# One list schedule over fixed buffers for a two-half state-space and convolution kernel

## The chip, the cores and the metric

The kernel runs on one core of a Trainium2 chip. The metric is the device time of one execution in microseconds (us), the median of several runs. One more execution is taken with the hardware profiler; its rows are what is read below.

## The reference

The input `x` is 2048 tokens of 640 channels. Four layers follow one another, each on a layer-normalised `x` and added to `x`:

```python
x = x + _A_ref(_layernorm(x), ...)   # A1
x = x + _B_ref(_layernorm(x), ...)   # B1
x = x + _A_ref(_layernorm(x), ...)   # A2, same weights as A1
x = x + _B_ref(_layernorm(x), ...)   # B2, same weights as B1
# _A_ref: h_t = Lam_bar * h_(t-1) + B_bar u_t (complex, 640 states); y = 2 Re(C h) + Dskip * u
# _B_ref(q, k, v): kv = shift_conv4(k) * v; y = causal_conv(kv, ssm_k) + ssm_D * kv; return q * y
```

In `_B_ref` only `q` depends on `x`. The long convolution `y` depends on the inputs `B_k`, `B_v`, `B_ssm_k` alone, so it is computed once and used by B1 and B2.

## The kernel before

The program has two halves. The first half builds everything that does not depend on `x`; the second half is the four layers.

**First half.** `a_setup_tasks` makes the weights of the A layers: `BT0` (the input matrices transposed, by ten DMA transposes, `e_bt0`, L379 and L380), `BT1` (the same times a diagonal, 100 matmuls and 10 evacuations), `W0`, `W1` (20 small products from transposed `C`, L444 and L445) and `G0` (five products of 10 x 640 columns, L464). The diagonals `Ld`, `Fd` and `DS` are made on VectorE, one 128 x 128 block at a time (L327, L429, L845). `y_table_tasks` makes sine and cosine tables, `kv_tasks` the product `kv` (stored in DRAM as `kvd`), and `y_pass` the convolution of one fifth of the channels (`qd` = 0 to 4): two transforms in two stages each (A: L908, B: L930 to L935) for the kernel (`KA`, `KB`) and for `kv` (`VA`, `VB`), six products on VectorE (L984 to L989), two stages back (`IB`: L1008 and L1009, a DMA transpose L1021, `IA`: L1036), and a store to DRAM as `ysd`.

**Second half.** Tokens come in four chunks of 512. `ALayer.chunk` does one chunk of an A layer: mean and variance (`ln_stats`: row sums L1182, squares L494), normalisation into `u` (L511 on ScalarE or L513 on VectorE), a DMA transpose into `uT` (L538), 100 matmuls of 256 columns into `ab` (L553, L556, evacuated at L562), rotation (L575 to L577), two scans (L591), rotation back into `h` (L614 to L616), four output groups of matmuls (L636, 33,280 columns in all), and one VectorE operation each that adds the residual and sums the row (`e_xe`, L641). `b_chunk` does one chunk of a B layer: statistics, normalisation into `bu`, product with `Y` (L665), addition to `x` with the row sum (L667), or into `o` for the output (L670).

**What sets the order.** Each half is a list of tasks with an engine, an estimated cost and dependencies. `Sched.run` is a list scheduler that puts them into an order by rank. It runs once for each half, and the program is emitted in that order; the framework's own scheduler may still move instructions. Buffers are rings of tiles in memory pools. The pools of the first half are closed before those of the second half are opened over the same memory, so no tile of the second half can be written before the first half's tiles there are done with. All DMAs are issued from the SP queue, in one order.

Of the kernel before, what the change touches and what calls it, by code (L numbers as in the profile page):

```python
# [43 lines left out]
QORD = [0, 16] + list(range(1, 16))  # L44
QGRP = [(0, 4), (4, 8), (8, 12), (12, 16), (16, 17)]


class Task:
    __slots__ = ("name", "engs", "ests", "eng", "est", "deps", "emit", "idx", "start", "finish", "rank", "succ", "bias", "lat", "uses")

    def __init__(self, name, eng, est, deps, emit, idx, bias, lat, uses):
# [5 lines left out]
        self.start = self.finish = None  # L57
        self.rank = 0.0
        self.succ = []
        self.bias, self.lat = bias, lat  # L60
        self.uses = uses


class Slot:
    __slots__ = ("tile", "users", "ring", "left", "vis", "held", "num")

    def __init__(self, ring, num):
        self.num = num
# [12 lines left out]

class Ring:

    def __init__(self, bufs, alloc, in_order=True):
        self.alloc = alloc
        self.avail = [0.0] * bufs
        self.in_order = in_order
        self.made = self.given = 0

# [5 lines left out]
class Sched:  # L95
    LAT = {"pe": 0.2, "act": 0.25, "dve": 0.2, "pool": 0.3, "sp": 2.2, "xp": 2.0}

    debug = False

    def __init__(self):  # L100
        self.tasks = []

    def add(self, name, eng, est, deps, emit, bias=0.0, lat=None, uses=()):
        t = Task(name, eng, est, deps, emit, len(self.tasks), bias, lat, list(uses))
        for s in t.uses:
            s.users += 1
        self.tasks.append(t)
        return t

    def vis(self, d):  # L110
        return d.finish + (d.lat if d.lat is not None else self.LAT[d.eng])

    def run(self):
        tasks = self.tasks
        for t in tasks:
# [16 lines left out]
        eps = 1e-9  # L132

        def can(t):
            if rtime[t.idx] > now + eps:
                return False
            need = {}
            for s in t.uses:
                if not s.held:
                    need[s.ring] = need.get(s.ring, 0) + 1  # L140
                    if s.ring.in_order and s.num != s.ring.given + 1:
                        return False
            for r, n in need.items():
                if sum(1 for a in r.avail if a <= now + eps) < n:
# [3 lines left out]
        while len(order) < len(tasks):  # L148
            progressed = False
            for eng in sorted(eng_free):  # L150
# [39 lines left out]
        for t in order:  # L190
            t.emit(t.eng)
        span = max(t.finish for t in tasks)
        if self.debug:
            self.report(order, span)
        return span

    def report(self, order, span):
        engs = sorted({t.eng for t in order})
        print("[sched] span %.1f" % span, {e: round(sum(t.est for t in order if t.eng == e), 1) for e in engs})
        bk = 10.0  # L200
        for b in range(int(span / bk) + 1):
            row = []
            for e in engs:
                o = sum(max(0.0, min(t.finish, (b + 1) * bk) - max(t.start, b * bk)) for t in order if t.eng == e)
                row.append("%s %3.0f" % (e, 100 * o / bk))
            print("   %5.0f  " % (b * bk) + "  ".join(row))


def c_mm(n, k=1):
    return k * (n / 2400.0 + 0.003)  # L210


def c_act(n, sb=False):
    return (0.25 if sb else 0.22) + 0.00083 * n


def c_tt(n, slow=False):
    return 0.15 + (0.00104 if slow else 0.00053) * n
# [16 lines left out]
def make_consts(nc, pool):  # L235
# [5 lines left out]
    for nm, v in (("half_pi", HALF_PI), ("neg_pi", -PI_LO), ("pos_pi", PI_LO)):  # L241
# [9 lines left out]
def a_setup_tasks(S, nc, wp, sp, R_ps, consts, A_Lambda_re, A_Lambda_im, A_B_re, A_B_im, A_C_re, A_C_im, A_log_dt, A_Dskip):  # L251
# [12 lines left out]
    st = {}  # L264

    def tl(nm, shape, dt=F32):
        return sp.tile(shape, dt, tag=nm, name=nm)

    s_pp = R_ps.new()

    def e_pl(_):
        st["pb"] = tl("pl_b", [4 * NJ, P], BF)
        for v, vec in enumerate((A_Lambda_re, A_Lambda_im, A_log_dt, A_Dskip)):
            nc.sync.dma_start(out=st["pb"][NJ * v:NJ * (v + 1), :], in_=vec.rearrange("(j p) -> j p", p=P))
    t_pl = S.add("a_pl", "sp", 0.3, [], e_pl, bias=3000)

    def e_pt(_):
        pf = tl("pl_f", [4 * NJ, P])
        nc.vector.tensor_copy(pf[:], st["pb"][:])
        ps = s_pp.get()  # L280
        nc.tensor.transpose(ps[:, 0:4 * NJ], pf[:], consts["ident_f"][0:4 * NJ, 0:4 * NJ])
        st["pf"] = tl("pl", [P, 4 * NJ])
        nc.vector.tensor_copy(st["pf"][:], ps[:, 0:4 * NJ])
# [954 lines left out]
```

## Time and profile before

| | |
|---|---|
| median of 3 runs | 463.53 us (460.25 to 464.36) |
| the profiled execution | 462.58 us, of which the span from the first to the last instruction is 460.6 us |
| mean granted clock of TensorE | 0.914 of full speed |
| busy: PE, DVE, ACT, POOL | 349.6, 323.9, 244.9, 6.9 us |

In the rows PE is TensorE, PEld its weight load, DVE is VectorE, ACT is ScalarE, POOL is GpSimd and SP is the engine that issues DMAs; L12 is line 12 of the kernel. A row of the stretches gives for each engine the busy time in that stretch, then the granted clock and the share of the DMA engines.

### The profile page before, as it was taken

The page shows a single profiled execution, that of the slowest core. Times are in us where ns is not written, and L with a number is a line of the kernel's source. Part 1 is how long each engine was busy: PE and PEld are TensorE (multiplying, and loading weights), DVE is VectorE, ACT ScalarE, POOL GpSimd, SP SyncE. Part 2 cuts the span into 40 slices and gives each one's busy share as a digit, 9 for nine tenths or more (in the row PEclk, how much of TensorE's full clock was granted, in tenths as well). Part 3 has the DMA queues.
Part 4 walks back from the last instruction along what each step waited for, and adds up shares of the span by engine and source line. Part 5 has one row for each costly group of instructions (what it writes and reads, how often), then busy time and mean ns, then how long its engine had stood idle before and what let it go on. Part 6 is the DMA issues. An engine that isn't in the chain of part 4 may idle for free.

```text
span 460.6 us, 7946 instructions
## 1 busy us (share of the span) xinstructions
PE 349.6 (76%) x3303; PEld 256.2 (56%) x3330; DVE 323.9 (70%) x595; ACT 244.9 (53%) x380; POOL 6.9 (1%) x21
## 2 busy tenths in 40 slices
PE   0386777989888796049799529999997698999920
PEld 0153466988777653038645318876574475855510
DVE  4995657688787630022997715999699899699674
ACT  3643457889888451962203779521737453430734
POOL 5000000000000000000000000000000000000000
PEclk9998989999999799559989958999998699999985
DMA  6999995929735668051002153301301313030021
GB/s 143 249 177 240 237 218 98 178 49 193 144 60 112 129 115 280 30 96 20 0 1 58 43 128 58 58 1 58 59 1 57 57 58 58 2 114 1 30 85 57
DMA packets 118173, 43.25 MB, mean 94 GB/s; under 512 B 112117, under 2 KB 113402, under 8 KB 118138
## 3 DMA queue, kind: packets, MB, share of 16 engines
q1 hardware_dynamic: 118138, 42.75, 41.8%
q8 instruction: 26, 0.43, 0.4%
q14 instruction: 9, 0.07, 0.1%
HBM read 14.76 MB, written 7.86 MB: 49 GB/s over the span
## 4 chain that ended last, share of the span: by engine, by line
DVE 38%; ACT 13%; PE 13%; DMA 5%; issue 2%; ACTq 0%; SPq 0%
DVE g L591 10%; ACT junk L494 8%; DVE x L641 4%; PE ps L464 3%; DMA xb<-in_A_x_dram 3%; DVE bu L665 2%; PE ps L553 2%; DVE t L575 2%; DVE o L670 2%; DVE g L577 2%; DVE t L615 2%; DVE t L614 2%; DVE t L576 2%; DMA uT<-u 2%; PE ps L556 2%; DVE x L667 2%
## 5 line engine op out<-in xcount | busy, mean ns | idle before, releaser
L636 PE MATMUL ps<-W,h 128*128 128x512 bf16 (+1 forms) x632 | 98.1, 304 | 6.4 <-DVE h L616 5.9
L223 ACT ACTIVATE q<-ps 128x1024 bf16<-128x1024 f32 (+2 forms) x81 | 75.4, 1003 | 42.8 <-PE ps L935 19.2
L553 PE MATMUL ps<-uT,BT 128*128 128x256 bf16 x400 | 61.1, 287 | 42.1 <-DMA uT<-u 41.8
L494 ACT ACTIVATE junk<-x,nmean 128x640 bf16<-128x640 f32 x48 | 39.7, 827 | 75.9 <-DVE nmean L488 61.4
L636 PEld LDWEIGHTS <-h 128*128 128x128 bf16 x640 | 50.2, 99 | 42.6 <-DVE h L616 6.9
L553 PEld LDWEIGHTS <-BT 128*128 128x128 bf16 x400 | 40.8, 103 | 49.6 <-issue 22.7
L556 PE MATMUL ps<-uT,BT 128*128 128x256 bf16 x400 | 60.1, 284 | 0.0
L591 DVE TENSOR_TENSOR_SCAN g<-rtab,g 128x1290 bf16<-128x1290 f32 x16 | 44.8, 2833 | 0.0
L556 PEld LDWEIGHTS <-BT 128*128 128x128 bf16 x400 | 40.8, 102 | 6.1
L225 DVE CAST q<-ps 128x1024 bf16<-128x1024 f32 (+2 forms) x34 | 30.4, 929 | 17.2 <-PE ps L1009 10.4
L511 ACT ACTIVATE bu<-x,nmr,rstd 128x640 bf16<-128x640 f32 x26 | 23.5, 915 | 28.2 <-DVE x L667 18.4
L930 PE MATMUL ps<-q,Cf 128*128 128x128 bf16 x170 | 35.6, 222 | 3.5 <-DVE vT L872 2.8
L933 PE MATMUL ps<-q,NSf 128*128 128x128 bf16 x170 | 35.8, 222 | 0.0
L562 ACT ACTIVATE ab<-ps 128x1024 bf16<-128x1024 f32 (+1 forms) x24 | 20.8, 871 | 24.5 <-PE ps L556 24.4
L935 PE MATMUL ps<-q,Cf 128*128 128x128 bf16 x150 | 33.2, 221 | 0.0
L932 PE MATMUL ps<-q,Sf 128*128 128x128 bf16 x150 | 33.2, 221 | 0.0
L866 PE MATMUL ps<-kT,DS 128*128 128x512 bf16 x78 | 21.4, 431 | 14.4 <-DVE DS L845 11.3
L908 PE MATMUL ps<-FA,qx 128*128 128x256 bf16 x160 | 21.5, 276 | 9.1 <-DMA qx<-kvd 2.4
L636 PEld LDWEIGHTS <-uT 128*128 128x128 bf16 x240 | 19.8, 99 | 13.7 <-issue 0.5
L636 PE MATMUL ps<-G,uT 128*128 128x128 bf16 (+1 forms) x151 | 26.8, 297 | 0.5
L908 PEld LDWEIGHTS <-qx 128*128 128x128 bf16 x160 | 15.6, 99 | 13.9 <-issue 9.0
L866 PEld LDWEIGHTS <-DS 128*128 128x128 bf16 x80 | 8.5, 107 | 26.0 <-DVE DS L845 12.4
(218 smaller groups left out, 652.1 us busy)
## 6 DMA issues: line engine op xcount, KB each, us to landing
Y<-ysd SPq DMA_DIRECT2D x8, 640.0 KB
qx<-in_B_ssm_k_dram SPq DMA_DIRECT2D x5, 512.0 KB
kvd<-vT SPq DMA_DIRECT2D x5, 512.0 KB, 4.5
qx<-kvd SPq DMA_DIRECT2D x5, 512.0 KB, 4.7
ysd<-yq SPq DMA_DIRECT2D x5, 512.0 KB
xb<-in_A_x_dram SPq DMA_DIRECT2D x4, 640.0 KB, 4.0
out_dram<-o SPq DMA_DIRECT2D x8, 320.0 KB, 2.2
Bnat<-in_A_B_re_dram SPq DMA_DIRECT2D x1, 800.0 KB, 6.7
```

Source lines behind the costliest of these rows:

```text
L223: nc.scalar.activation(out, in_, ACT.Copy)
L225: nc.vector.tensor_copy(out, in_)
L494: nc.scalar.activation(junk[:], src(q), ACT.Square, bias=st["nmean"][:, q:q + 1], scale=1.0, accum_out=st["ssq"][:, q:q + 1])
L553: nc.tensor.matmul(pb[:, jj, c2, :], lhsT=aw["BT1"][:, c2, j, k, :], rhs=uT[:, k, 0:2, :].rearrange("p t i -> p (t i)"), start=(k == 0), s ...
L556: nc.tensor.matmul(pb[:, jj, c2, :], lhsT=aw["BT0"][:, c2, k, j * P:(j + 1) * P], rhs=uT[:, k, 2:4, :].rearrange("p t i -> p (t i)"), star ...
L591: nc.vector.tensor_tensor_scan(gv, rt, gv, 0.0, ALU.mult, ALU.add)
L636: nc.tensor.matmul(pc[:, o0:o1], lhsT=lh, rhs=rh, start=(n == 0), stop=(n == len(ops) - 1))
L908: nc.tensor.matmul(pa[:, o4, :], lhsT=s_x.get()[:, 4 * g + o4, :], rhs=T["FA"][:], start=True, stop=True)
L930: nc.tensor.matmul(ps[:, g, 0, :], lhsT=T["Cf"][:, q, :], rhs=are, start=True, stop=single)
L932: nc.tensor.matmul(ps[:, g, 0, :], lhsT=T["Sf"][:, q, :], rhs=A[:, 2 * q + 1, :], start=False, stop=True)
L933: nc.tensor.matmul(ps[:, g, 1, :], lhsT=T["NSf"][:, q, :], rhs=are, start=True, stop=single)
L935: nc.tensor.matmul(ps[:, g, 1, :], lhsT=T["Cf"][:, q, :], rhs=A[:, 2 * q + 1, :], start=False, stop=True)
```

## The change

- **One schedule.** All tasks of both halves go into one `Sched`. Its order is emitted under `manual_schedule()`, which keeps it as it is on each engine. The tasks of the first half have larger ranks (`S.base`), so a layer task goes ahead only where they leave an engine free.
- **Fixed buffers.** Nearly all tiles are views of 13 buffers of 2580 bf16 (`b5`) and 6 of 2580 f32 (`b10`), which are allocated once and shared by both halves. A ring now has a store and a cap; the scheduler picks the buffer.
- **Weights by PE.** `BT0` comes from 50 matmuls with the identity and 10 evacuations. The two `B` matrices and the first `ssm_k` are loaded by DMAs of the ACT queue.
- **GpSimd** makes the diagonals `Ld`, `Fd`, `DS`, `DD` (one operation for many blocks), the short chain of factors, and the tables `FA`, `HA`.
- **A1 residual on PE.** For A1, `x` is loaded a second time (`xr`, one buffer) and added by one more identity matmul per column part (16 x 640 columns). The row sum with the copy to `x` can then be on ACT or DVE.
- **Layer norm.** The mean and the standard deviation are scaled on ACT (L524, L534) and no longer on DVE. The last chunk of B2 is normalised one row group at a time.

```diff
 class Ring:
-    def __init__(self, bufs, alloc, in_order=True):
-        self.alloc = alloc
-        self.avail = [0.0] * bufs
+    def __init__(self, store, cap, view, in_order=True):
+        self.store, self.cap, self.view, self.in_order = store, cap, view, in_order
...
-        for t in order:
-            t.emit(t.eng)
...
+        with self.tc.manual_schedule():
+            for t in order:
+                t.emit(t.eng)
...
+    def diag(dst, scal, n):
+        nc.gpsimd.tensor_tensor(dst, ident[:, None, :].to_broadcast([P, n, P]), scal[:, :, None].to_broadcast([P, n, P]), ALU.mult)
...
-            nc.sync.dma_start_transpose(out=aw["BT0"][:, 0, k, :], in_=A_B_re[:, k * P:(k + 1) * P])
-            nc.sync.dma_start_transpose(out=aw["BT0"][:, 1, k, :], in_=A_B_im[:, k * P:(k + 1) * P])
...
+                for j in range(NJ):
+                    nc.tensor.matmul(pb[:, j, :], lhsT=s_B[c].get()[:, j, k * P:(k + 1) * P], rhs=ident[:], start=True, stop=True)
...
-        nc.vector.tensor_scalar(st["nmean"][:], sums(), -1.0 / D, None, ALU.mult)
+        nc.scalar.activation(st["nmean"][:], sums(), ACT.Copy, scale=-1.0 / D)
...
+        if reload is not None:
+            res_slot = reload[0]
+            t_xr = S.add(f"{nm}_xr", "sp", 0.4, [t_bp], reload[1], uses=[res_slot], xt=3.0)
...
+                    if reload is not None:
+                        ops = ops + [(ident[:], resid(q)[:, d0:d1], d0, d1)]
...
+                if reload is not None and eng == "act":
+                    nc.scalar.activation(s_x.get()[:, q, :], s_pc.get()[:, 0:D], ACT.Identity, accum_out=sums_out()[:, q:q + 1])
...
-        S.run()
-        early.close()
-
-
-    S = Sched()
-    with ExitStack() as a:
...
+        "b5": store(wp, NB5, "b5", [P, 2 * NJ * NC2], BF),
+        "b10": store(wp, 6, "b10", [P, 2 * NJ * NC2], F32),
...
+        "q1": Ring(b10, 2, lambda t: bfv(t, NQ * 2 * DQ)),
+        "q2": Ring(b10, 2, lambda t: bfv(t, NQ * 2 * DQ)),
+        "q3": Ring(b10, 2, lambda t: bfv(t, NQ * 2 * DQ)),
...
+        "xb": Ring(b5, 2, v4),
+        "xr": Ring(b5, 1, v4),
...
+        groups = [range(4)] if c < NCH - 1 else [[0], [1], [2], [3]]
```

The order of ScalarE where the two halves meet. Before, the last evacuations of `G` (a weight) and `yq` (the last convolution output) stand ahead of the first row sum of `xb` (chunk 0 of `x`):

```order
L223 ACTIVATE G_98<-ps 128x640
L223 ACTIVATE yq<-ps 128x16x64
L223 ACTIVATE G_98<-ps 128x640 x4
L1182 ACTIVATE junk,sums<-xb 128x640 x5
L494 ACTIVATE junk,ssq<-xb,nmean 128x640 x4
```

After, where the same weight `G` is evacuated (names that begin with `b_` are shared buffers; `b_5_87` holds chunk 0 of `x`, `b_1_96` and `b_5_100` hold spectra of the second and third fifth, `b_2_84` the first fifth's output):

```order
L240 ACTIVATE G_114<-ps_103 128x640
L1236 ACTIVATE junk,sums_1188<-b_5_87 128x640 x4
L524 ACTIVATE nmean_0_1215<-sums_1188 128x4
L529 ACTIVATE junk,ssq_0_1216<-b_5_87,nmean_0_1215 128x640
L240 ACTIVATE G_114<-ps_106 128x640
L529 ACTIVATE junk,ssq_0_1216<-b_5_87,nmean_0_1215 128x640 x3
L240 ACTIVATE b_1_96<-ps_106 128x1024
L240 ACTIVATE b_1_96<-ps_105 128x256
L534 ACT_TABLE_LOAD
L534 ACTIVATE std_0_1293<-ssq_0_1216,eps 128x4
```

The statistics of A1's chunk 0 now stand ahead of the evacuations of four of the five fifths of the convolution.

The order of VectorE at the end of the convolution. Before, from the last of the six products of the last fifth to the first rotation of A1 (`t<-ab`):

```order
L989 TENSOR_TENSOR q_2207<-q_2207,q_2147 128x2176
L429 TENSOR_SCALAR Fd<-ident_bf,F_578 128x128 x4
L225 CAST q_2304<-ps 128x8x32x4
L225 CAST q_2304<-ps 128x2x32x4
L225 CAST W_97<-ps 128x640
L429 TENSOR_SCALAR Fd<-ident_bf,F_578 128x128 x6
L225 CAST W_97<-ps 128x640
L225 CAST yq<-ps 128x16x64
```

After, the same place (`b_0_82` holds `ab` of chunk 0, `b_8_90` its scan, `b_5_100` the last fifth's inverse):

```order
L1048 TENSOR_TENSOR b_3_98<-b_3_98,b_2_97 128x2176
L611 TENSOR_TENSOR b_4_99<-b_0_82,tab 128x10x256
L612 TENSOR_TENSOR b_4_99<-b_0_82,tab 128x10x256
L613 TENSOR_TENSOR b_8_90<-b_4_99 128x10x256
L615 MEMSET b_8_90 128x10
L242 CAST b_5_100<-ps_104 128x8x32x4
L539 RECIPROCAL rstd_2_2457<-std_2_2314 128x4
L541 TENSOR_TENSOR nmr_2_2459<-nmean_2_2136,rstd_2_2457 128x4
L242 CAST b_5_100<-ps_105 128x6x32x4
L627 SCALAR_TENSOR_TENSOR b_8_90<-rtab,b_8_90 128x1290 x2
```

The rotation and the scan of A1's chunk 0 moved up to directly behind the last six products, among the last evacuations of the convolution.

The order of SP's queue in the layers, after (L1231 is the second load of `x` for the residual, L575 the transpose into `uT`, L1247 the load of `Y`; the four transposes shown are A1's chunk 3 and A2's chunks 0 to 2):

```order
L575 DMA_TRANSPOSE b_5_87<-b_12_94 128x20x128
L1231 DMA b_11_93<-in_A_x_dram 128x2x1280
L1247 DMA b_7_89<-ysd 128x2x1280
L1231 DMA b_9_91<-in_A_x_dram 128x2x1280
L575 DMA_TRANSPOSE b_0_82<-b_10_92 128x20x128
L1247 DMA b_4_86<-ysd 128x2x1280
L1231 DMA b_10_92<-in_A_x_dram 128x2x1280
L575 DMA_TRANSPOSE b_1_83<-b_11_93 128x20x128
L1247 DMA b_3_85<-ysd 128x2x1280
L575 DMA_TRANSPOSE b_7_89<-b_6_88 128x20x128
```

Before, there are no second loads in this place, and a transpose stands behind loads of `Y` alone; now A2's first two transposes stand behind a load of `xr` too, which has one buffer.

## Rows read from the trace of the kernel before

**Rows 1.** The page: busy time, share of the span, instructions of each engine.

```profile
PE 349.6 (76%) x3303; PEld 256.2 (56%) x3330; DVE 323.9 (70%) x595; ACT 244.9 (53%) x380; POOL 6.9 (1%) x21
```

**Rows 2.** Stretches of the span: length; busy PE, PEld, DVE, ACT, POOL; clock, DMA.

```profile
0.00:19.00 19.00, 0.91 (x5) 0.73 (x5) 12.78 (x63) 10.85 (x15) 6.55 (x18) 1.00 0.86 184
19.00:66.70 47.70, 36.65 (x271) 22.18 (x274) 33.33 (x112) 19.78 (x25) 0.34 (x3) 0.93 1.07 218
66.70:147.10 80.40, 72.28 (x1095) 65.51 (x1098) 62.61 (x74) 68.85 (x80) 0.00 (x0) 1.00 0.61 121
147.10:180.40 33.30, 27.98 (x272) 18.91 (x274) 13.65 (x23) 14.85 (x20) 0.00 (x0) 0.90 0.71 161
180.40:231.00 50.60, 25.32 (x204) 21.19 (x206) 18.71 (x26) 24.00 (x45) 0.00 (x0) 0.76 0.22 57
231.00:440.00 209.00, 185.34 (x1444) 126.84 (x1461) 170.74 (x277) 98.15 (x184) 0.00 (x0) 0.93 0.19 48
440.00:460.60 20.60, 1.11 (x17) 0.82 (x14) 12.06 (x26) 8.38 (x14) 0.00 (x0) 0.65 0.16 64
```

**Rows 3.** The waits, longest in total first: us, times, longest.

```profile
ACT junk L494 <- DVE nmean L488: 62.7, 9, 22.2
PE ps L553 <- DMA uT<-u: 41.8, 5, 22.0
```

**Rows 4.** The timeline where the halves meet: start, length, idle before and releaser.

```profile
180.46 0.70 ACT L223 ACTIVATE G<-ps 128x640 bf16<-128x640 f32 x1 [2.13 <-PE ps L468]
184.68 0.74 ACT L1182 ACTIVATE junk<-xb 128x640 bf16<-128x640 bf16 x1 [3.51 <-DMA xb<-in_A_x_dram]
202.36 1.23 PE L553 MATMUL ps<-uT,BT 128*128 128x256 bf16 x5 [22.00 <-DMA uT<-u]
231.00 4.00 PE L636 MATMUL ps<-W,h 128*128 128x512 bf16 x10 [3.27 <-DVE h L616]
```

**Rows 5.** Groups by line and form: busy, mean ns of one, idle before.

```profile
L591 DVE TENSOR_TENSOR_SCAN g<-rtab,g 128x1290 bf16<-128x1290 f32 x16 | 44.8, 2833 | 0.0
L494 ACT ACTIVATE junk<-x,nmean 128x640 bf16<-128x640 f32 x48 | 39.7, 827 | 75.9 <-DVE nmean L488 61.4 <-DVE g L586 10.5 <-DVE nca L604 3.0
L641 DVE SCALAR_TENSOR_TENSOR x<-ps,xb 128x640 f32<-128x640 f32 x16 | 12.9, 814 | 0.9 <-PE ps L636 0.9
L575 DVE TENSOR_TENSOR t<-ab,tab 128x2560 bf16<-128x2560 bf16 x8 | 11.9, 1492 | 15.5 <-ACT ab L562 15.5
L223 ACT ACTIVATE BT<-ps 128x640 bf16<-128x640 f32 x9 | 6.1, 721 | 0.2 <-PE ps L393 0.2
L429 DVE TENSOR_SCALAR Fd<-ident_bf,F 128x128 bf16<-128x128 bf16 x30 | 5.5, 249 | 0.0
L845 DVE TENSOR_SCALAR DS<-ident_bf,skf 128x128 bf16<-128x128 bf16 x20 | 4.1, 251 | 3.4 <-PE ps L866 3.4
L327 DVE TENSOR_SCALAR Ld<-ident_bf,lam 128x128 bf16<-128x128 bf16 x15 | 2.5, 253 | 0.0
```

**Rows 6.** The timeline: matmuls of 256 columns that follow one another.

```profile
208.47 0.71 PE L556 MATMUL ps<-uT,BT 128*128 128x256 bf16 x5
209.02 0.71 PE L553 MATMUL ps<-uT,BT 128*128 128x256 bf16 x5
```

**Rows 7.** One densely filled stretch of the layers, columns as in Rows 2.

```profile
300.00:400.00 100.00, 90.96 (x720) 64.66 (x726) 90.57 (x140) 43.65 (x78) 0.00 (x0) 0.95 0.17 40
```

**Rows 8.** DMA issues: bytes of one, median us from issue to landing.

```profile
xb<-in_A_x_dram SPq DMA_DIRECT2D x4, 640.0 KB, 4.0
uT<-u SPq DMA_TRANSPOSE x8, 4.9
```

**Rows 9.** The timeline of the first microseconds: GpSimd alone, and beside VectorE.

```profile
1.29 0.81 POOL L708 IOTA kq<- 128x768 f32 x1
9.38 1.39 POOL L708 IOTA kq<- 128x640 f32 x1 [4.95 <-DVE xc L712]
10.10 1.09 DVE L711 TENSOR_SCALAR xs<-kq,pidx 128x768 int32<-128x768 f32 x1
```

More of the change, by code (lines that the diff above doesn't have):

```diff
@@ L131, in run @@
         now = 0.0
-        eps = 1e-9
         def can(t):
@@ L189, in run, with c_ts @@
         order.sort(key=lambda t: (t.start, t.idx))
-        for t in order:
-            t.emit(t.eng)
[L192 to L206, printed above, removed]
+        with self.tc.manual_schedule():
+            for t in order:
+                t.emit(t.eng)
 def c_mm(n, k=1):
-    return k * (n / 2400.0 + 0.003)
+    return k * (n / 2400.0 + 0.0028)
 def c_act(n, sb=False):
-    return (0.25 if sb else 0.22) + 0.00083 * n
+    return (0.22 if sb else 0.19) + 0.00083 * n
 def c_tt(n, slow=False):
-    return 0.15 + (0.00104 if slow else 0.00053) * n
+    return (0.16 if slow else 0.13) + (0.00104 if slow else 0.00053) * n
+def c_ts(n=P):
+    return 0.08 + n / 960.0
 def evac(nc, eng, out, in_):
@@ L264, in a_setup_tasks @@
     st = {}
+    v = nc.vector
+    ident = aw["ident"] = consts["ident_bf"]
     def tl(nm, shape, dt=F32):
-        return sp.tile(shape, dt, tag=nm, name=nm)
-    s_pp = R_ps.new()
[L271 to L283, printed above, removed]
@@ L1073 @@
     nc = tc.nc
-    wp = ctx.enter_context(tc.tile_pool(name="weights", bufs=1))
+    wp = ctx.enter_context(tc.tile_pool(name="fixed", bufs=1))
     psp = ctx.enter_context(tc.tile_pool(name="psum", bufs=1, space=PSUM))
@@ new lines, in store @@
+    def store(pool, n, nm, shape, dt):
+        return Store([pool.tile(shape, dt, tag=f"{nm}_{i}", name=f"{nm}_{i}") for i in range(n)])
+    St = {
+        "b5": store(wp, NB5, "b5", [P, 2 * NJ * NC2], BF),
+        "b10": store(wp, 6, "b10", [P, 2 * NJ * NC2], F32),
+        "fd": store(wp, 2, "fd", [P, 6 * P], BF),
+        "ps": store(psp, 4, "ps", [P, 1024], F32),
+    }
+    St["s_par"] = Ring(St["b5"], 1, lambda t: t[:]).new()
+    R_ps = St["R_ps"] = Ring(St["ps"], 4, lambda t: t[:], in_order=False)
@@ new lines, in y_load, with e_yl @@
+    def y_load(c):
+        s_Y = R["Y"].new()
+        def e_yl(_, c=c, s_Y=s_Y):
+            nc.sync.dma_start(out=s_Y.get().rearrange("p (t q) d -> p t (q d)", t=2), in_=tok_view(ysd, c))
+        return s_Y, S.add(f"yl{c}", "sp", 0.4, y_stores, e_yl, uses=[s_Y], xt=3.0)
+    for c in range(NCH):
+        s_Y, t_y = y_load(c)
+        s_x = xslots[c]
+        rd = b_chunk(S, nc, R, small, c, "B1", s_x, lambda c=c: su(1, c), ready[c], s_Y, t_y, lambda c=c: su(2, c), None, [range(4)])
+        ready[c] = A2.chunk(c, lambda q, s=s_x: s.get()[:, q, :], lambda c=c: su(2, c)[:], rd, lambda q, s=s_x: s.get()[:, q, :],
+                            s_x, lambda c=c: su(3, c), s_x, None)
@@ L1211 @@
+    for c in range(NCH):
+        s_Y, t_y = y_load(c)
+        groups = [range(4)] if c < NCH - 1 else [[0], [1], [2], [3]]
+        b_chunk(S, nc, R, small, c, "B2", xslots[c], lambda c=c: su(3, c), ready[c], s_Y, t_y, None, out[0], groups)
+    S.run()
 _INS = ['A_x', 'A_Lambda_re', 'A_Lambda_im', 'A_B_re', 'A_B_im', 'A_C_re', 'A_C_im', 'A_log_dt', 'A_Dskip', 'B_q', 'B_k', 'B_v', 'B_shift_k', 'B_ssm_k', 'B_ssm_D']
```

974 lines of the change are left out of this document (492 added, 482 removed).

## The prediction, made before the changed kernel ran

> **What bounds the kernel now.** I read the busy line first [rows 1]. No engine is full: TensorE is busy for 76% of the span, VectorE for 70%, ScalarE for 53%. So the time is lost between stages, and the table of stretches says where [rows 2]. Its seven stretches are cut at events: the first kv matmul (19.0), the first and the last of the five spectral products (66.7 and 147.1), the last `G` evacuation (180.4), the first output matmul of A1 with `h` (231.0), and the last matmuls (440).
>
> Three stretches stand out. From 147.1 to 180.4 VectorE works 13.65 of 33.3 us. From 180.4 to 231.0 TensorE works 25.32 of 50.6 us, VectorE 18.71, ScalarE 24.00, at a mean clock of 0.76 of full speed. In the last 20.6 us TensorE has nothing left. The middle one is the wall between the halves: the last weight is evacuated at 180.46, and only then is `x` loaded; the first row sum starts at 184.68, the first A1 matmul at 202.36 after 22.00 us of idle TensorE, the first matmul with `h` at 231.00 [rows 4]. The longest waits are the same story: squares that wait for a mean, 62.7 us, and matmuls that wait for the transpose `uT`, 41.8 us [rows 3]. In the layers the engine that fills up is VectorE: 90.57 of 100 us between 300 and 400, with TensorE at 90.96 [rows 7], whose busy time is modelled and overlaps itself. A 256-column matmul costs 0.55/5 = 0.11 us there at full clock (208.47 to 209.02 for five) [rows 6].
>
> **The change, part by part.** I make the sum against the profiled execution, 462.58 us, of which 460.6 are the span, so 2.0 lie around it. It stands 1.0 us under the median. I cut the new time at the first A1 matmul with `h` (231.0 before) and call that moment T.
>
> *Work before T.* By 231.0 VectorE has done 12.78 + 33.33 + 62.61 + 13.65 + 18.71 = 141.1 us and ScalarE 10.85 + 19.78 + 68.85 + 14.85 + 24.00 = 138.3, together 279.4 [rows 2].
> - The diagonals go to GpSimd: 5.5 + 4.1 + 2.5 = 12.1 us less [rows 5]. The table and factor operations that go there too are short; I count them as nothing.
> - `BT0` by matmuls: 50 x 128 = 6,400 columns on TensorE, at 0.11 us for 256 some 2.7 us, in the first 20 us, where TensorE is idle anyway (0.91 of 19 us busy), so free. The 10 evacuations cost 10 x 0.721 = 7.2 us [rows 5]. If the early cover were gone, all of this would be 10 us. The ten DMA transposes leave a stretch where the DMA engines are full (share 1.07 from 19 to 66.7) [rows 2]; I count no gain.
> - The statistics of A1's chunks 2 and 3 now stand ahead of T: 24 passes (a sum, a square, a normalisation for each of 8 row groups), and three evacuations of chunk 2, which I count as four passes more: 28 at 0.83 us [rows 5], 23 us.
>
> The sum is 279.4 - 12.1 + 7.2 + 23 = 297.5 us for two engines that mostly share it, 148.8 each. How well are they filled? From 66.7 to 147.1 the two are busy (62.61 + 68.85) / 160.8 = 82% [rows 2], in a stretch with the same transforms. I take that for the whole: 148.8 / 0.82 = 181.5. Two corrections. The first 19 us are filled to only (12.78 + 10.85) / 38 = 62%, which costs 19 x 0.20 = 4. In the new order 17 evacuations of `W` follow one another on ScalarE and then five products for `G`, with VectorE nearly out of work; half of that imbalance, 10 us, I add. **T = 196**, against 231. The bounds of the fill: 0.88 gives 183, 0.75 gives 212. TensorE isn't in the way: the columns up to T (five fifths of 34,816, kv 40,960, weights 71,000 and 6,400, three chunks of 25,600) make 369,000, at 0.11 us for 256 some 159 us.
>
> *From T to the end.* VectorE works 170.74 + 12.06 = 182.8 us after 231 [rows 2]. Fourteen of A1's sixteen residual additions (L641, 0.814 us each) are on ScalarE in the new order: 11.4 less, 171.4 left [rows 5]. ScalarE has the room, with 98.15 of 209 us [rows 2]. TensorE has four A1 outputs and one A1 input, then all of A2: 8 x 33,280 + 5 x 25,600 + 10,240 for the new residual matmuls = 404,500 columns, 174 us. So VectorE and TensorE are near each other, and I take the fill of the dense stretch, 0.906 [rows 7]: 171.4 / 0.906 = 189, and 3 us for the last store. **192**, against 229.6. Bounds: at the old mean fill (182.8 / 229.6 = 0.80) it is 217; at 0.95 it is 183. What lets it be dense: `x` of the later chunks is loaded early, so their A1 input no longer waits, and the tail is cut, since the last chunk of B2 is normalised by rows as they come. What is late next is VectorE itself: its scans alone are 2.83 us each [rows 5].
>
> *Residual on TensorE.* 10,240 columns are 4.4 us, inside the 174. The reload takes 4.0 us [rows 8] on SP's queue. What is queued behind a reload that waits is the transpose `uT` of an A2 chunk (4.9 us [rows 8]), in two places of the new order. I count nothing, because TensorE has at least one chunk's output (14 us) between; the price if not is below.
>
> *GpSimd.* The trace of before shows no arithmetic of that size there. The nearest rows are index fills: 0.81 us for 768 elements alone, 1.05 ns an element, and 1.39 us for 640 while VectorE ran, 2.17 ns, with VectorE's own operation at 1.09 us meanwhile [rows 9]. Some 12,900 elements go there (2,300 + 500 for the tables, 640 + 2,560 + 1,920 + 3,840 for diagonals, the fills), so 13.5 to 28 us in the first 60. I take the lower end, as hidden: the first `DS` must be there when the first `kT` is, which was at 19 us before, and at either rate some 5,100 elements stand ahead of it. The upper end goes into the range, as +10.
>
> The Trainium skill speaks against this part: its page "GPSIMD Engine Reference", section "3.1 Elementwise — side-by-side cycle accounting", gives 4497 ns for a two-input operation of 2048 elements on GpSimd and 2293 on VectorE, and keeps elementwise work on VectorE. By its figure the 12,900 elements would be an estimated 28 us, the upper end above; the fill beside a busy VectorE agrees with it, the one alone doesn't.
>
> **Sum.** 196 + 192 + 2 = **390 us**, 16% under 463.5.
>
> **The rivals.**
> - *GpSimd late.* The diagonals come at 2.17 ns an element, `Ld` and `Fd` hold up the weights' products in TensorE's fixed order, and VectorE is slowed beside them. 390 + 10 = 400. For it: the slow fill. Against it: the products have conv matmuls ahead of them.
> - *The layers stay as loose as now.* The chain statistics, `uT`, matmuls, scan, matmuls is what it was, and with VectorE filled to 0.80 the layers take 217: 196 + 217 + 2 = 415. For it: 62.7 us of waits for a mean [rows 3] are a chain's, not only a wall's. Against it: 100 us of 0.906.
> - *The wall stays.* Nineteen shared buffers replace larger pools. If A1's first chunk finds no free buffer until the tables are done with, T is 231: 231 + 192 + 2 = 425. Against it: the new order has A1's statistics ahead of four fifths of the convolution.
> - *Denser than I think.* Fill 0.88 before T and 0.95 after it: 183 + 183 + 2 = 368.
> - *The queue, on the slow side.* In SP's queue A2's transposes stand behind `xr`, which has one buffer and waits for the last matmul of the A1 chunk ahead, or behind a load of `Y`, which waits for a buffer. If the wait there comes last, TensorE stands idle for the transpose (4.9) and for VectorE's way to `h` (six operations of 1.49 and two scans of 2.83, 14.6 us [rows 5, 8]), about 20 a chunk. For all four: 390 + 80 = 470, slower than before. It decides from the fourth: three give 450. For it: one order of one queue with no second choice. Against it: between each pair of such waits the order gives TensorE another chunk's matmuls.
>
> **How the numbers follow.** A change of under 1% can't be told from none in this kernel (its runs lie between 460.25 and 464.36). Chances: forecast 390 0.46, layers loose 415 0.20, GpSimd late 400 0.12, denser 368 0.09, wall 425 0.06, queue 470 0.07. The range of 374 to 430 leaves out most of the denser case and the queue. Faster by over 1% (below 459): the first five, 0.93, less 0.01 for an unlucky wall; of the queue's 0.07, 0.02 is within 1% and 0.05 slower; with that 0.01, slower is 0.06.
>
> **What would show it.** In the profile of the changed kernel: the first A1 row sum at about 80 to 95 us, long before the last convolution matmul; no stretch of 20 us without TensorE before the end; the first matmul with `h` near 196; VectorE over 88% busy from there to the end; the last matmul within 12 us of the end. If GpSimd is late, the first kv matmul comes after 21 us and matmuls of `W` wait for `fd`. If the queue decides, L553 again heads the waits with `uT`. I am wrong if ScalarE and VectorE in the convolution are filled much less than 82%, for instance because four of the six large buffers (two hold `B` until `G` is made) let only one fifth run at a time, or if engines in the fixed order wait for each other by turns where the estimates were off.

## The result, and the profile after

The changed kernel takes 424.75 us (median of 4 runs, 424.33 to 426.24) against 462.19 for the kernel before in the same call (460.25 to 464.36): a ratio of 0.9195, 95% interval 0.9140 to 0.9249. The forecast was 390, with a range to 430. The profiled run took 424.33 us, 422.6 of them the span.

The busy line of the page after, to be read against [rows 1]:

```profile
PE 350.3 (83%) x3412; PEld 259.5 (61%) x3412; DVE 319.0 (75%) x430; ACT 251.5 (60%) x432; POOL 43.5 (10%) x81
```

The busy times of TensorE, VectorE and ScalarE are nearly the same (GpSimd works 37 us more, beside them), and the span is 38 us shorter: what is gone is idle time. The table of stretches of the changed kernel shows where idle time is left (columns as in [rows 2]). It is cut at these events: 77 and 111 frame the last weights and `G`, 197 is the end of the convolution's matmuls but for its last 32, 217.6 the first A1 matmul with `h`, 341 to 353 a hole, 402 nearly the last matmuls. The last two rows are sums over the time before and after 217.6.

```profile
0.00:19.00 19.00, 5.50 (x46) 4.73 (x46) 8.09 (x29) 7.32 (x12) 16.54 (x42) 1.00 0.83 193
19.00:77.00 58.00, 50.06 (x520) 38.32 (x521) 50.84 (x68) 41.42 (x55) 20.06 (x35) 0.97 0.80 160
77.00:111.00 34.00, 28.55 (x181) 15.00 (x180) 4.82 (x5) 17.09 (x31) 6.92 (x5) 0.95 0.52 129
111.00:197.00 86.00, 76.55 (x1117) 70.56 (x1116) 74.28 (x70) 80.62 (x130) 0.00 (x0) 1.00 0.67 140
197.00:217.60 20.60, 15.72 (x143) 12.82 (x141) 20.22 (x23) 8.05 (x11) 0.00 (x0) 0.83 0.73 169
217.60:341.00 123.40, 122.90 (x1012) 85.10 (x1011) 99.11 (x137) 68.80 (x139) 0.00 (x0) 1.00 0.24 60
341.00:353.00 12.00, 0.36 (x3) 0.26 (x2) 11.83 (x14) 0.00 (x0) 0.00 (x0) 0.69 0.00 0
353.00:402.00 49.00, 49.00 (x382) 31.63 (x380) 32.91 (x59) 21.02 (x47) 0.00 (x0) 0.97 0.09 28
402.00:422.60 20.60, 1.66 (x19) 1.12 (x17) 16.87 (x32) 7.20 (x13) 0.00 (x0) 0.62 0.35 127
0.00:217.60 217.60, 176.38 (x2001) 141.43 (x2002) 158.25 (x193) 154.50 (x234) 43.51 (x81) 0.97 0.70 151
217.60:422.60 205.00, 173.92 (x1412) 118.11 (x1410) 160.71 (x238) 97.03 (x198) 0.00 (x0) 0.94 0.20 55
```

The wall between the halves is gone: TensorE works 15.72 of the 20.6 us at which the convolution ends and the layers take over, where it had 25.32 of 50.6 [rows 2]. Idle time is left in three other places. From 77 to 111 VectorE works 4.82 of 34 us. From 217.6 to 341 TensorE is full (122.90 of 123.4 us), and then comes a hole of 11.64 us. Behind the last matmul, which ends at 403.66, 18.9 us pass without one, in which VectorE catches up on products and additions of B2.

Three of the rows of the waits after (columns as in [rows 3]):

```profile
ACT nmean L524 <- DVE b L690: 45.9, 5, 22.8
DVE rstd L539 <- ACT std L534: 24.4, 6, 6.1
PE ps L589 <- DVE b L690: 11.6, 1, 11.6
```

The third is the hole, and so is the longest wait of the first (22.8 us, until 354.13). VectorE's timeline says why (L690 is a residual addition of A2, L611 to L652 the product with the table, the scan and the product that makes `h`, of one chunk):

```profile
335.91 0.82 DVE L690 SCALAR_TENSOR_TENSOR b<-ps,b 128x640 f32<-128x640 f32 x1
336.65 0.08 DVE L690 DVE_READ_ACCUMULATOR b<-ps,b 128x1 f32 x1
336.65 1.49 DVE L611 TENSOR_TENSOR b<-b,tab 128x2560 bf16<-128x2560 bf16 x1
...
341.44 5.58 DVE L627 TENSOR_TENSOR_SCAN b<-rtab,b 128x1290 bf16<-128x1290 f32 x2
...
350.36 1.50 DVE L652 TENSOR_TENSOR b<-b 128x2580 bf16<-128x2580 bf16 x1
351.78 0.82 DVE L690 SCALAR_TENSOR_TENSOR b<-ps,b 128x640 f32<-128x640 f32 x1
```

And TensorE's:

```profile
340.30 0.72 PE L678 MATMUL ps<-W,b 128*128 128x128 bf16 x10
352.66 1.23 PE L589 MATMUL ps<-b,BT 128*128 128x256 bf16 x5 [11.64 <-DVE b L690]
353.68 1.27 PE L592 MATMUL ps<-b,BT 128*128 128x256 bf16 x5
354.75 1.27 PE L589 MATMUL ps<-b,BT 128*128 128x256 bf16 x5
```

The kernel has four PSUM buffers, into which TensorE writes its results. All four hold finished outputs of A2, and the additions that would free them stand in VectorE's fixed order behind 15 us of another chunk's rotation and scan. So TensorE's next matmul has no buffer and waits. When it resumes, the granted clock is 0.50, the lower level of 1.2 GHz (a stretch from 352.6 to 355.8 in the same view), and groups of five 256-column matmuls start 1.07 us apart instead of the 0.55 of [rows 6].

### The profile page after: what moved, and what is told of

It reads as the page before. It is cut to its first block, busy times and chain, and to the rows that moved or that the text cites. A ratio compares the mean times of both kernels' runs of the same rounds, so it can differ in the third digit from the quotient of the medians.

```text
span 422.6 us, 8138 instructions
## 1 busy us (share of the span) xinstructions
PE 350.3 (83%) x3412; PEld 259.5 (61%) x3412; DVE 319.0 (75%) x430; ACT 251.5 (60%) x432; POOL 43.5 (10%) x81
## 4 chain that ended last, share of the span: by engine, by line
PE 39%; DVE 36%; ACT 10%; DMA 7%; issue 5%; POOL 2%; POOLq 0%; SPq 0%; DVEq 0%; ACTq 0%
PE ps L678 13%; DVE b L627 5%; PE ps L589 5%; PE ps L592 5%; ACT junk L529 5%; DMA b<-b 5%; DVE b L242 4%; PE ps L500 3%; DVE b L716 3%; DVE b L714 3%; PE ps L922 2%; PE ps L1067 2%; PE ps L1068 2%; DVE b L718 2%; PE ps L964 2%
## 5 line engine op out<-in xcount | busy, mean ns | idle before, releaser
L240 ACT ACTIVATE b<-ps 128x1024 bf16<-128x1024 f32 (+3 forms) x106 | 90.9, 909 | 27.5 <-PE ps L592 16.1
L678 PEld LDWEIGHTS <-b 128*128 128x128 bf16 x880 | 67.7, 98 | 48.9 <-issue 0.6
L678 PE MATMUL ps<-W,b 128*128 128x128 bf16 (+1 forms) x640 | 95.8, 299 | 0.0
L589 PE MATMUL ps<-b,BT 128*128 128x256 bf16 x400 | 59.4, 281 | 15.2 <-DVE b L690 11.6
L242 DVE CAST b<-ps 128x1024 bf16<-128x1024 f32 (+2 forms) x43 | 48.7, 1162 | 15.1 <-PE ps L1068 6.2
L592 PE MATMUL ps<-b,BT 128*128 128x256 bf16 x400 | 58.5, 278 | 0.0
L529 ACT ACTIVATE junk<-b,nmean 128x640 bf16<-128x640 f32 (+1 forms) x64 | 52.9, 827 | 1.6
L627 DVE TENSOR_TENSOR_SCAN b<-rtab,b 128x1290 bf16<-128x1290 f32 x16 | 44.6, 2832 | 0.2
L548 ACT ACTIVATE b<-b,nmr,rstd 128x640 bf16<-128x640 f32 (+1 forms) x38 | 32.6, 911 | 15.7 <-DVE nmr L541 15.7
L524 ACT ACTIVATE nmean<-sums 128x4 f32<-128x4 f32 (+1 forms) x19 | 3.9, 203 | 59.3 <-DVE b L690 45.9
L986 PE MATMUL ps<-b,b 128*128 128x128 bf16 x170 | 35.1, 219 | 0.9 <-ACT b L240 0.6
L989 PE MATMUL ps<-b,b 128*128 128x128 bf16 x170 | 35.2, 219 | 0.0
L991 PE MATMUL ps<-b,b 128*128 128x128 bf16 x150 | 32.8, 219 | 0.0
L988 PE MATMUL ps<-b,b 128*128 128x128 bf16 x150 | 32.8, 219 | 0.0
L678 PE MATMUL ps<-G,b 128*128 128x512 bf16 (+1 forms) x160 | 27.0, 299 | 0.5 <-DVE b L690 0.5
L964 PEld LDWEIGHTS <-b 128*128 128x128 bf16 x160 | 15.7, 101 | 7.2 <-issue 4.4
L1067 PE MATMUL ps<-b,b 128*128 128x128 bf16 x160 | 18.8, 219 | 1.5 <-DVE b L928 0.8
```

Source lines behind the costliest of these rows:

```text
L240: nc.scalar.activation(out, in_, ACT.Copy)
L242: nc.vector.tensor_copy(out, in_)
L529: nc.scalar.activation(small.junk, src(q), ACT.Square, bias=st["nmean"][:, i:i + 1], scale=1.0, accum_out=st["ssq"][:, i:i + 1])
L589: nc.tensor.matmul(pb[:, jj, c2, :], lhsT=aw["BT1"][:, c2, j, k, :], rhs=uT[:, k, 0:2, :].rearrange("p t i -> p (t i)"), start=(k == 0), s ...
L592: nc.tensor.matmul(pb[:, jj, c2, :], lhsT=aw["BT0"][:, c2, k, j * P:(j + 1) * P], rhs=uT[:, k, 2:4, :].rearrange("p t i -> p (t i)"), star ...
L627: nc.vector.tensor_tensor_scan(gv, rt, gv, 0.0, ALU.mult, ALU.add)
```

## The experiments

All ratios are to the kernel before. Line numbers of edited kernels can differ by a few from those of the changed kernel.

**1. The wall put back (e1).**

```diff
-        t_xl = S.add(f"xl{c}", "sp", 0.4, [stores[-1]], e_xl, ...
+        t_xl = S.add(f"xl{c}", "sp", 0.4, y_stores, e_xl, ...
```

> Undone: the loads of x for A1 wait for the stores of all five fifths of the convolution, as in the kernel before; nothing else is changed by hand. Theory (the gain is the overlap of the halves): in the kernel before it took 50.5 us from the last evacuation of G to the first h matmul (180.46 to 231.00), so the first h matmul, now at 217.6, should come at 235 to 255 and the end at 440 to 462. Rival (the gain comes from less work and denser layers, the overlap only moves idle time): the end stays at 425 to 435.

Measured: 475.24 us, ratio 1.0297 (1.0268 to 1.0327), slower than the kernel before. TensorE stands idle for the first transpose again, as before [rows 4]:

```profile
225.95 1.25 PE L589 MATMUL ps<-b,BT 128*128 128x256 bf16 x5 [24.59 <-DMA b<-b]
267.27 1.24 PE L678 MATMUL ps<-G,b 128*128 128x512 bf16 x4
267.30:472.60 205.30, 173.37 (x1397) 118.27 (x1411) 163.92 (x240) 97.04 (x198) 0.00 (x0) 0.94 0.20 55
```

The first `h` matmul comes at 267.3, 49.9 us later than in the changed kernel, and the end 50.5 later: in this arrangement the overlap is worth all of that. What follows the first `h` matmul takes 205.3 us, as in the changed kernel (205.0), against 229.6 before: that part of the gain isn't the overlap's. And the wall alone doesn't explain a kernel slower than before. The first operation of each of the five spectral products shows where that time went. The row's "66.7 to 147.1" are the starts of the first and the last of the five; the rows are those of before, after and e1:

```profile
L984 DVE TENSOR_TENSOR q<-q,q x5: 1293/1293/1293, 66.7 to 147.1; 128x2176 bf16<-128x2176 bf16 x5
```

```profile
L1043 DVE TENSOR_TENSOR b<-b,b x5: 1281/1292/1293, 53.7 to 177.7; 128x2176 bf16<-128x2176 bf16 x5
```

```profile
L1043 DVE TENSOR_TENSOR b<-b,b x5: 1281/1283/1293, 53.4 to 178.0; 128x2176 bf16<-128x2176 bf16 x5
```

The convolution starts 13 us earlier and ends 31 us later, with or without the layers beside it. So the slower convolution belongs to the new arrangement itself, not to the layers that run beside it.

**2. Two large buffers given back to the convolution, behind the wall (e5).** `B` holds two of the six large buffers from its load until `G`. Here it is loaded once more for `G`, when `W` is there, and the weights rank 50 lower (no run takes these two apart).

```diff
+    s_G = [R_mat.new(), R_mat.new()]
+    t_gl.append(S.add(f"a_ldG{i}", "sp", 0.5, ws, e_lg, xt=3.2, uses=[s_G[i]]))
-    ... lhsT=s_B[c].get()[:, j, ksl] ... uses=[s_pg] + s_B
+    ... lhsT=s_G[c].get()[:, j, ksl] ... uses=[s_pg] + s_G
-    S.base = 9900.0
+    S.base = 9850.0
```

> The wall of e1, and B is loaded a second time for G once W is made, so that its two large buffers are free for the convolution meanwhile; the weights rank 50 lower. In e1 the last spectral product still comes at 178.0, against 147.1 in the kernel before, with no layer beside it. Theory (B's two of six large buffers throttle the convolution): last product at 130 to 152, first h matmul at 222 to 242, end 430 to 450. Rival (the fixed order, GpSimd or the block of W and G slows the convolution, not the buffers): last product at 170 to 180, end 465 to 478.

Measured: 439.98 us, 0.9486 (0.9438 to 0.9534), 35 us less than e1. The row for the products:

```profile
L1049 DVE TENSOR_TENSOR b<-b,b x5: 1280/1292/1293, 53.8 to 141.3; 128x2176 bf16<-128x2176 bf16 x5
```

The last product is 36.7 us earlier. With the wall up, this release and the lower rank of the weights together are what the convolution lacked; which of the two it is stays open. The first `h` matmul comes at 234.4, 3 us later than in the kernel before, and 205.5 us follow. So this kernel, in which the halves don't overlap, is already 23 us faster than the one before (463.14 in the same call). That gain lies behind the first `h` matmul and needs no overlap.

**3. The same without the wall, with the additions of A2 first (e8), beside the additions alone (e2).**

```diff
-            ... [t_cp], e_xe, uses=[s_pc, s_x]))
+            ... [t_cp], e_xe, bias=100.0 if reload is None else 0.0, uses=[s_pc, s_x]))
```

> Only the residual additions of A2 (L690) get a bias of 100 in the list, so that VectorE takes them as soon as their matmuls are done; the order is the same up to 341 us. Theory (the hole of 11.64 us in TensorE at 341 to 353 is made by VectorE's fixed order, which puts a chunk's L611 to L652 ahead of the additions that free the four PSUM buffers): the hole goes and is not made up for later, 410 to 415. Rival (VectorE has as much to do in all, so its chain is only late at another place): 421 to 426.

> e2's bias on the additions of A2, and B loaded a second time for G with the weights ranked 50 lower, as in e5, without the wall. Theory (TensorE must be full earlier than at 204 for a gain; with two buffers more the convolution is done earlier and A1's matmuls come earlier): 394 to 404 against e2's 409.9. Rival (the convolution's own pace is hidden behind A1's statistics and the weights): 407 to 413.

Measured: e2 409.94 us, 0.8886 (0.8853 to 0.8919); e8 409.75, 0.8842 (0.8801 to 0.8883). e2 confirms the cause of the hole: its profiled span is 14.7 us shorter. That is nearly the 11.64 us, some 1.6 us that TensorE lost at half clock behind it, and a tail 1.0 us shorter. Here are stretches of e2 over the place of the hole and the last 17.9 us:

```profile
341.00:353.00 12.00, 12.00 (x106) 9.62 (x105) 11.86 (x15) 3.27 (x8) 0.00 (x0) 1.00 0.00 1
353.00:390.00 37.00, 36.70 (x290) 22.38 (x293) 35.24 (x58) 18.51 (x40) 0.00 (x0) 1.00 0.10 33
390.00:407.90 17.90, 0.00 (x0) 0.00 (x0) 14.44 (x28) 4.13 (x8) 0.00 (x0) 0.57 0.42 153
```

e8 refutes its theory: its last product comes at 141.7, as in e5, yet the first `h` matmul stays at 217.8, and nothing is gained over e2. The block of `G` has moved to 180 to 194, where VectorE works 1.46 us of 14:

```profile
141.30:180.00 38.70, 26.64 (x264) 20.64 (x266) 20.84 (x24) 27.85 (x49) 4.29 (x2) 0.87 0.78 169
180.00:194.00 14.00, 13.89 (x107) 8.10 (x107) 1.46 (x4) 12.91 (x26) 0.00 (x0) 1.00 0.52 163
```

VectorE and ScalarE together are filled to 71% up to 217.8, as in the changed kernel (72%). The idle time went to another place. Beside e5, which has the wall but not the bias, e8 has the first `h` matmul 16.5 us earlier: with the buffers released, the overlap moves it by a third of the 49.9 us of e1.

**4. Chunk 0's output ahead of chunk 2's input (e3).**

```diff
-            t_bp = S.add(f"{nm}_bp{gi}", ..., [t_tu] + AT["bt"], ...
+            t_bp = S.add(f"{nm}_bp{gi}", ..., [t_tu] + AT["bt"] + (self.gate if c == 2 and reload is not None else []), ...
+            if c == 0:
+                self.gate = [t_cp]
```

> One dependency added: the input matmuls of A1's chunk 2 wait for the output matmuls of chunk 0. It also raises the rank of all that leads to chunk 0's output, so the list differs from about 45 us on. Theory (TensorE's fixed order puts chunk 2's input, which waits for a late transpose, ahead of chunk 0's output, whose h was ready at 202): first h matmul at 198 to 206, end at 410 to 418. Rival (the work ahead of it on ScalarE and VectorE sets that moment, or what is put back there comes late further on): first h matmul at 212 or later, or end within 421 to 427.

Measured: 426.40 us, 0.9223 (0.9164 to 0.9283); no difference to the changed kernel. The first `h` matmul did come at 202.7, 14.7 us earlier, and the hole is where it was:

```profile
202.71 0.61 PE L678 MATMUL ps<-W,b 128*128 128x512 bf16 x1
352.82 1.22 PE L589 MATMUL ps<-b,BT 128*128 128x256 bf16 x5 [11.65 <-DVE b L692]
```

Between 204 and 217 TensorE has no gap in either kernel; chunk 2's input now comes behind the output instead of ahead of it, and the matmul behind the hole starts at 352.8 instead of 352.7. **The first `h` matmul isn't a milestone of the time.** What the two kernels share is that TensorE is full from about 204 on (but for a gap of 3.2 us in e3), and that the hole ends at the same moment.

**5. The residual on TensorE (e4, e6, e7).** e4 undoes it; e6 leaves its matmuls out, so that nothing adds `x` there; e7 keeps them and moves the 14 evacuations of ScalarE to VectorE.

```diff
 e4, e6:
-                    if reload is not None:
-                        ops = ops + [(ident[:], resid(q)[:, d0:d1], d0, d1)]
 e4:
-                if reload is not None and eng == "act": ... (evacuation with a row sum on ScalarE or VectorE)
+                nc.vector.scalar_tensor_tensor(... resid(q), ALU.mult, ALU.add, accum_out=...)   # all 16
 e7:
-                if reload is not None and eng == "act":
+                if False:
```

> Undone: A1's residual on TensorE. The 10,240 columns are left out, and all sixteen additions are done by VectorE from the reloaded x, at the places in the list at which 14 stood on ScalarE. Theory after the trace (TensorE sets the pace of the layers, 122.9 us busy of 123.4 from 217.6 to 341): 4.4 us less for TensorE, of which 0 to 4 come through, 419 to 425. Rival, as I predicted it (VectorE sets the pace of the layers): 11.4 us more on VectorE, 428 to 436.

> A1's residual is left out (its 32 identity matmuls on TensorE are taken away, nothing adds x), the order of everything else is the same. It prices these matmuls alone. Theory (TensorE sets the pace from 204 on): 4.4 us less on TensorE come through whole or nearly, 419.5 to 422. Rival (VectorE sets it): 423.5 to 426.

> The 14 evacuations of A1's outputs that stand on ScalarE (L686) are issued on VectorE (L688) at the same places in the list; the residual stays on TensorE and x's buffer is held as long as before. 14 times 0.90 us more for VectorE. Theory (TensorE sets the pace, and e4 lost its 12.7 us to the one buffer of the reloaded x, which was held longer): 424 to 428. Rival (VectorE sets the pace, e4 is explained by its 11.4 us): 432 to 438.

Measured: e4 437.45 us, 0.9483 (0.9453 to 0.9512); e6 422.98, 0.9141 (0.9112 to 0.9169); e7 434.51, 0.9387 (0.9357 to 0.9418). Of TensorE's 4.4 us some 1.8 come through in e6. Of VectorE's 12.6 us more in e7 (14 times 0.90) 9.8 do. My reading of the trace, that TensorE alone sets the pace, falls, and so does my guess in e7's expectation that e4 lost its time to the buffer of `x`. e4 holds that buffer longer and has another order, so the price isn't taken from it. In e7 TensorE waits for VectorE ahead of the hole and in it:

```profile
314.19 0.71 PE L589 MATMUL ps<-b,BT 128*128 128x256 bf16 x5 [1.92 <-DVE b L688]
...
346.14 0.59 PE L678 MATMUL ps<-G,b 128*128 128x512 bf16 x1 [5.81 <-DVE b L690]
...
362.02 1.23 PE L589 MATMUL ps<-b,BT 128*128 128x256 bf16 x5 [10.07 <-DVE b L690]
```

In the changed kernel TensorE is full until 341, yet VectorE's order decides when the hole ends. Of the work that e6 takes from TensorE ahead of it, more than half comes back as a longer hole, now in two pieces:

```profile
334.82 0.58 PE L676 MATMUL ps<-G,b 128*128 128x512 bf16 x1 [3.75 <-DVE b L688]
350.70 1.22 PE L589 MATMUL ps<-b,BT 128*128 128x256 bf16 x5 [10.19 <-DVE b L688]
```

Work given to VectorE moves the end of the hole, from 352.7 to 362.0 in e7.

**6. Diagonals on VectorE (e9), BT0 by DMA (e11).**

```diff
 e9:
-        nc.gpsimd.tensor_tensor(dst, ident[:, None, :]...      # and the same for kv's
+        nc.vector.tensor_tensor(dst, ident[:, None, :]...
 e11:
-                    nc.tensor.matmul(pb[:, j, :], lhsT=s_B[c].get()[:, j, k * P:(k + 1) * P], rhs=ident[:], ...)
-                evac(nc, eng, aw["BT0"][:, c, k, :], s_pb.get()[:, 0:D])
+                nc.sync.dma_start_transpose(out=aw["BT0"][:, c, j, :], in_=...)      # behind each of W's
```

> Undone: the diagonals (L343, L899) are made by VectorE instead of GpSimd, as whole operations at the same places in the list; the order of everything else is the same. Theory (GpSimd's 18 us for them are hidden, and VectorE, which is nearly idle from 80 to 100 us and waits for TensorE's evacuations before 22 us, hides them as well): 422.5 to 427. Rival (GpSimd is late: matmuls wait for fd): first kv matmul before 21 us, end at 412 to 420. Rival on the other side (VectorE is slowed where it is needed): 428 to 434.

> Undone: BT0 comes by ten DMA transposes on SP's queue, each issued behind one of W's transposes; its 50 matmuls and 10 evacuations are left out of the list's places, the order of everything else is the same. Theory from the trace (in the first 22 us TensorE's fixed order starts with BT0's matmuls, which wait 11.86 us for B, and VectorE waits 9.50 us for their first evacuation, so the tables and the first kv matmul at 23.4 come late): first kv matmul at 18 to 20, end 2 to 5 us earlier, 420 to 423. Rival as I predicted it (BT0 on TensorE is free): 424 to 426. Rival on the other side (the transposes delay W or kv): 427 or more.

Measured: e9 427.18 us, 0.9230 (0.9205 to 0.9255); e11 427.67, 0.9247 (0.9216 to 0.9278). The medians are 2.4 and 2.9 us above the changed kernel's, with intervals that overlap its own. GpSimd is hidden: in e9 the first kv matmul comes at 23.23 instead of 23.43, although VectorE makes a 128x512 diagonal block in 685 ns and GpSimd in 1049. In e11 it comes at 22.7, so BT0's wait for `B`, 11.86 us at the head of TensorE's order, isn't what holds it up either: my theory there falls. In TensorE's order twelve other matmuls stand ahead of the first of kv. In e11 they wait for an addition on VectorE (L1012 there, L1013 in the changed kernel), and that one waits for its own load:

```profile
18.91 1.20 DVE L1012 TENSOR_TENSOR b<-b,kd 128x16 bf16<-128x16 bf16 x1 [4.06 <-DMA b<-in_B_ssm_k_dram]
20.16 2.74 PE L963 MATMUL ps<-FA,b 128*128 128x256 bf16 x12 [4.62 <-DVE b L1012]
22.70 3.48 PE L921 MATMUL ps<-b,fd 128*128 128x512 bf16 x9
```

The first diagonals need a copy that stands behind the same addition. The ten transposes stand in SP's queue: a load of `k` that was issued at 56.94 us is issued at 60.01 in e11. No run shows that BT0 on TensorE costs more than what it replaced.

**7. The list without the fixed order (e10).**

```diff
-        with self.tc.manual_schedule():
-            for t in order:
-                t.emit(t.eng)
+        for t in order:
+            t.emit(t.eng)
```

> The list is made as before and emitted without the block that fixes the order of instructions, so that the framework's own scheduler may move them. Theory (the list decides, fixing it costs or gives little): 420 to 432. Rival (the fixed order is what makes the change fast): 440 or more. Rival on the other side (the fixed order is what makes engines wait by turns): 415 or less.

Measured: 433.42 us, 0.9387 (0.9351 to 0.9423), between my theory and its rival. The spectral products run from 65.4 to 197.6 instead of 53.7 to 177.7, and the first `h` matmul is at 235.7; 195 us follow, 10 less than in the changed kernel. The hole is shorter, and so is the tail, 11.2 us instead of 18.9:

```profile
368.98 1.22 PE L588 MATMUL ps<-b,BT 128*128 128x256 bf16 x5 [6.12 <-DVE b L689]
419.80:431.00 11.20, 0.00 (x0) 0.00 (x0) 6.75 (x18) 4.46 (x10) 0.00 (x0) 0.65 0.23 88
```

Of the 10 us 7.7 are the tail's. Fixing the order gains 18 us up to the first `h` matmul and loses 10 behind it.

**8. A version of several changes (e12).** It has e2's bias; the weights ranked ahead of the convolution (`S.base = 10001.0`); and A1's residual on VectorE from the kept chunk of `x` (`xb` with three buffers, no reload). The bias goes to every layer without a reload, so here it reaches A1's additions as well as A2's.

> A version with three things: e2's bias on A2's additions; the weights ranked 101 higher, ahead of the convolution; A1's residual on VectorE, from the chunk's x that is kept (three buffers for it, none for a reload). Theory A (order decides, VectorE has room once it isn't waited for): 394 to 403. Theory B (each addition on VectorE costs as in e7, 9.8 us for 14): 407 to 418.

Measured: **402.23 us**, 0.8700 (0.8686 to 0.8714), the fastest here, 22.5 us under the changed kernel. Its page:

```profile
PE 338.9 (85%) x3356; PEld 253.2 (63%) x3380; DVE 326.8 (82%) x463; ACT 243.6 (61%) x399; POOL 41.9 (10%) x81
```

VectorE makes A1's additions here, and such work was dear in e7, yet this is the fastest version. The output matmuls with `h` start at 208.0 and run without a break to 250.6 over three chunks, and the largest gap of TensorE after that is 3.73 us:

```profile
207.96 1.24 PE L678 MATMUL ps<-G,b 128*128 128x512 bf16 x4
277.78 4.02 PE L678 MATMUL ps<-W,b 128*128 128x512 bf16 x10 [3.73 <-DVE b L652]
```

That the bias makes the additions cheap is a guess: the parts weren't run one by one, and what each gives stays open.

## Why the prediction was right, and why it was 35 us low

The direction and the range were right, and the wall did fall; e1 shows what putting it back costs. By my sum: 196 + 192 + 2; measured 217.6 + 205.0 + 1.7. Against 231.0 + 229.6 before, 13.4 us came ahead of the first `h` matmul, where I wanted 35, and 24.6 behind it, where I wanted 37.6. The 425 of the rival *the wall stays* is the time that was measured, but only by chance: the wall is gone, and both terms were too low for other reasons.

**The term T, 21.6 us too low.** Two things were mis-sized, work and fill (the busy share of VectorE and ScalarE together).
- Work: VectorE and ScalarE had done 158.25 + 154.50 = 312.75 us by then, not 297.5. The difference is the second A1 chunk's way to `h`, six operations of 1.49 and two scans of 2.83, 14.6 us, which I had put behind T. At a fill of 82% that is some 9 us of T.
- Fill: 82% held, and more, where only transforms ran: (74.28 + 80.62) / 172 = 90% from 111 to 197, which gave some 8 us back. It failed in the block of the last weights and `G`, 77 to 111: (4.82 + 17.09) / 68 = 32%. At 82% that block would have taken 13.4 us; it lost 20.6, and I had added 10. The first 19 us, filled to 41%, lost 9.6; I had added 4.

The reason that I gave for being wrong, `B` holding two of the six large buffers, is real but not the whole answer. With the wall up, freeing them (with the weights' lower rank) is worth 35 us (e5); without it, nothing (e8), where the block of `G` is idle time at another place. So the overlap and the buffers aren't two gains that add up. And T, as I chose it, bounds nothing (e3).

**The layers, 13 us too low.** TensorE's 174 us were right (173.92), and VectorE had 160.71, fewer than 171.4 by roughly what came ahead of T. The fill was 160.71 / 205 = 78%, not 0.906: the rival *the layers stay as loose as now* had the fill (0.80) nearly right, but not the cause. The missing time is one hole, 11.64 us, and a tail of 18.9 where I wanted less than 12. I gave two reasons why the layers would be dense. The first held: the A1 input no longer waits as it did before,

```profile
273.80 1.25 PE L553 MATMUL ps<-uT,BT 128*128 128x256 bf16 x5 [13.75 <-DMA uT<-u]
```

and TensorE waited for a `uT` only once, for 3.6 us. In e1 no such wait stands behind the first `h` matmul either, so this gain needs no overlap. The second failed: normalising the last chunk by row groups cut the tail only from 19.5 to 18.9 us. What I didn't see is that a fixed order with four PSUM buffers lets the evacuating engine block TensorE by doing the next chunk's work first (e2).

**The small terms.** *Residual on TensorE*: 4.4 us was right (in the changed kernel's timeline the two matmuls of an output take 0.27 to 0.28 us, 16 times), and in this order it pays: its matmuls cost 1.8 us (e6), and evacuations on VectorE would cost 9.8 (e7). Whether it pays in e12's order isn't known. *GpSimd*: hidden, as taken (e9), though the upper rate was the nearer one, and its work was 36.6 us more than before, not 13.5 to 28:

```profile
L343 POOL TENSOR_TENSOR fd<-ident_bf,s_F 128x768 bf16<-128x768 bf16 x5 | 7.6, 1531 | 19.4 <-PE ps L922 12.4 <-PE ps L419 7.0
```

That is 2.0 ns an element. The Trainium skill's "GPSIMD Engine Reference", section "3.1 Elementwise — side-by-side cycle accounting", has 4497 ns for a two-input operation of 2048 fp32 elements, an estimated 2.2 ns an element. The trace's bf16 operations come near it and lie below: 2.0 here, and 1.8 for the one of 1920 elements (3393 ns). The Trainium skill's advice there, to keep elementwise work on VectorE, would have cost what e9 measures, 2.4 us or nothing. *BT0*: near nothing either way (e11). *The queue*: SP waited up to 29.8 us for `u`, but TensorE had other matmuls in between, as argued.

**The signs.** First row sum at 106.86, not 80 to 95; the longest gap of TensorE 11.86, under 20; first `h` matmul at 217.4; VectorE 78% busy after it, not 88; last matmul 18.9 us before the end; first kv matmul at 23.4, which I had named as GpSimd's sign and which e9 shows is not.

## What to carry to other kernels

When halves of a kernel are overlapped, price the overlap and the buffers that it takes away apart: here the wall's fall gave 50 us, but in an arrangement that without it is 13 us slower than the kernel before, and with two buffers given back 23 us faster. In a fixed order, look in the fullest engine's timeline for its one or two long gaps and give the instruction that ends them a higher rank; a bias on one kind of task was worth 14.8 us. An earlier milestone was worth nothing where the engine behind it was full anyway (e3); an engine can be full for 120 us and still not be what decides the next gap.

## What the runs showed of the hardware

A DMA transpose holds the queue that issues it, a plain copy hardly: on SP some 1.25 us for a transpose of 128x640 and 2 to 5.5 for those of 128x2048, but 0.34 to 0.59 us for most copies of 512 and 640 KB (single ones take up to 3.5). Whether e11's 2.9 us, if they are real, come from that or from the DMA engines wasn't tried. Their share is 0.96 from 40 to 60 us and 1.10 from 60 to 80; in the changed kernel it is 1.10 and 0.71.
